# Batch 2's attention: strided head pairs in float32 groups first, then local head pairs in float16 units, on another timetable

## The chip, the core and the metric

The kernel runs on one core of one Trainium2 chip. The metric is the device time of one execution in microseconds (us), the median of several runs of the same program. The engines are TensorE (PE, with its weight loads as PEld), VectorE (DVE), ScalarE (ACT), GpSimd (POOL) and SyncE (SP), whose queue issues nearly all DMA transfers. Each works through its instructions in the order in which the program put them on it, and waits on semaphores for the others.

## The reference

Three stages follow each other, for 4 batches of 576 tokens and 512 channels:

```
scores = q @ k.T / 8                              # 8 heads of 64 channels
mask   = heads 0-3 (local):   0 <= row - col < 32
         heads 4-7 (strided): row >= col and row % 32 == col % 32
x = softmax(where(mask, scores, -1e9)) @ v        # heads side by side: 512 channels
h = relu(x @ w_in); u, v = halves of h            # gated unit
x = (u * (w_spatial @ layernorm(v) + b_spatial)) @ w_out
theta = x @ w_theta                               # token mixing
y = w_tok_r @ (x * cos(theta)) + w_tok_i @ (x * sin(theta))
u = x + y;  out = u + relu(u @ w_ch)
```

Results are float32. The kernel holds most operands as a pair of float16 numbers (a high part and what is left) and multiplies them in three passes.

## The kernel before

**The main line.** For each batch, `main_v` multiplies x with the second half of w_in (PSUM tiles `v`), `main_mid` makes `u`, `sp`, `x` and `th` chunks, and `main_end` makes `y` and `c` chunks and sends the output. The order is v(0), mid(0), v(1), end(0), mid(1), v(2), end(1), mid(2), v(3), end(2), mid(3), end(3). Main PSUM tiles come from a pool of three. A `y` chunk is 54 matmuls of 288 columns and there are four; two first `c` chunks follow with 18 matmuls each before their last 6.

**Attention.** Batch 0's stands ahead of the main line. The attention of batches 1, 2 and 3 is given out in steps between pieces of the main line: a generator yields after each step, and `others` (called after each piece) takes the next step of batch b once the main line's nominal clock, counted in matmul columns, has passed `ATT_AT[b][0] + n * ATT_AT[b][1]`. `drain(b + 1)` takes all that is left before `main_v(b + 1)`.

There are two forms of it:

- `attention1` (float32, batches 1 and 2 before): 9 groups g0 to g8 of up to 4 local or 6 strided blocks. g0 to g4 are the local head pairs 0 and 1, g5 to g8 the strided pairs 2 and 3. A group has scores and mask (into bank `sc`), row maximum and difference (DVE, `st` and `sm`), exponential (ACT), transposes by PE (bank `av`), a copy to SBUF (ACT, `pT`), the product with v (bank `av`), a division (DVE), transposes (bank `sc`) and two evacuations into xT (ACT, DVE). A step s does the output of group s-3, the product of s-2, the scores of s and the transposes of s-1.
- `attention` (float16 pairs, batch 3 before): 11 units of 4 blocks, 6 local and 5 strided. `prep_qk` loads one head's q and k for a pair as float32 (`qs`, `ks`, one buffer each) and splits them into `qT` and `kT`; `kT` lies in the same two tiles `kts` (`kt_80`, `kt_81` in the order) as the float32 form's q and k. A unit has scores (`sc`), four masked minimum passes (DVE), four exponentials (ACT), a division, a split into `ph`, one DMA transpose, and three steps later the product (`av`).

`sc` and `av` are one PSUM bank each for all groups and units. `vT` has two buffers, shared by the float32 v tiles (`v_...`) and the float16 ones.

**What else is in the way.** While batch 0's end runs, the weights w_ch are still being converted (`xT<-in_w_ch_dram`, ACT and DVE `wx`, POOL `wch`), batch 1's rows are normalised (`rs`, `vr`, `vn` on DVE and ACT), and the rotated values of batch 0 are transposed by DMA (`zf<-vn`). Main evacuations have a priority of 200 over attention work when a scheduler sets each engine's order; it is fixed in the program.

All instructions are recorded under one helper line (L103), so the rows below are told apart by tile names.

Of the kernel before, what the change touches and what calls it, by code (L numbers as in the profile page):

```python
# [32 lines left out]
N32 = 3  # L33
# [18 lines left out]
E_YHI = 'vaavvaav'  # L52
E_ZLO = 'vvvvvvvv'
WARM = 6
ATT_AT = (None, (2.7, 3.9), (79.0, 5.4), (169.9, 4.6))
CONV_SP = (20.0, 9.9, 1.9)
CONV_OUT = (37.0, 12.0, 5.0)
CONV_TH = (49.0, 12.0, 5.0)
# [7 lines left out]
def kernel(  # L66
# [52 lines left out]
    nc = Engines  # L119
    B, DM, S = out.shape  # L120
# [28 lines left out]
    def copy(eng, key, dst, src):  # L149
        e = eng[key]  # L150
        if key == "a":
            e.activation(dst, src, AF.Copy)
        else:
            e.tensor_copy(dst, src)
# [170 lines left out]
    units = []  # L325
# [4 lines left out]
    NU = len(units)  # L330
# [7 lines left out]
    def prep_qk(b, hp, j, tiles):  # L338
        local = hp < 2
        nk = S + STRIDE if local else S  # L340
        if j == 0:
            qT = att_p.tile([P, 2, S], F16, tag="qT", name="qT", bufs=2)
            kT = kts[hp % 2].rearrange("p j n -> p (j n)").bitcast(F16).rearrange("p (e j n) -> p e j n", e=2, j=2)
            tiles[hp] = qT, kT
        qT, kT = tiles[hp]
        qs = att_p.tile([P, S], F32, tag="qs", name="qs")
        nc.sync.dma_start(qs, qd[b - N32, hp, :, j, :])
        ks = att_p.tile([P, S + STRIDE], F32, tag="ks", name="ks")
        nc.sync.dma_start(ks[:, 0:nk], (kl_d[b - N32, hp] if local else ks_d[b - N32, hp - 2])[:, j, :])
        copy(N, E_QHI, qT[:, j], qs)  # L350
        nc.vector.tensor_tensor(qT[64:P, j], qs[64:P], qT[64:P, j], ALU.subtract)
        copy(N, E_KHI, kT[:, 0, j, 0:nk], ks[:, 0:nk])
        N[E_KLO].tensor_tensor(kT[:, 1, j, 0:nk], ks[:, 0:nk], kT[:, 0, j, 0:nk], ALU.subtract)

    def prep_v(ld):
        vs, nb = ld
        vT = att_p.tile([P, 2, 6, 2, 64], F16, tag="vT", name="vT", bufs=2)
        nc.scalar.activation(vT[:, 0, 0:nb], vs[:, 0:nb], AF.Copy, scale=VSC)
        nc.vector.scalar_tensor_tensor(vT[:, 1, 0:nb], vs[:, 0:nb], VSC, vT[:, 0, 0:nb],
                                       op0=ALU.mult, op1=ALU.subtract)  # L360
        return vT
# [65 lines left out]
    NG = len(groups)  # L427

    def load_qk(b, hp, q, k, c0, c1, by=None):
        by = by or nc.sync  # L430
        local = hp < 2
        src = kzl[b, hp] if local else kzs[b, hp - 2]
        k0, k1 = (c0 + STRIDE if c0 else 0, c1 + STRIDE) if local else (c0, c1)
        by.dma_start(q[:, c0:c1], qp[b, hp][:, c0:c1])
        for j in range(2):
            h = slice(64 * j, 64 * j + 64)
            by.dma_start(k[h, k0:k1], src[h, j, k0:k1])

    def load_vl(b, hp, v):
        src = vl_d[b, hp].rearrange("p n j d -> p n (j d)")  # L440
        c = slice(1, VW - 1)
        nc.gpsimd.memset(v[:, 0:9, 0:VW:VW - 1], 1.0)
        nc.sync.dma_start(v[0:96, 0:9:3, c], src[0:96, 0:6:2])
        nc.sync.dma_start(v[0:64, 1:9:3, c], src[64:128, 0:6:2])
        nc.sync.dma_start(v[64:96, 1:9:3, c], src[32:64, 1:6:2])
        nc.sync.dma_start(v[0:96, 2:9:3, c], src[32:128, 1:6:2])
# [211 lines left out]
            for f in end:  # L658
                f()

    def attention1(b):
        q, k, v = {}, {}, {}

        def load_a(hp):
            q[hp], k[hp] = kts[hp % 2][:, 0], kts[hp % 2][:, 1]
            load_qk(b, hp, q[hp], k[hp], 0, S)

        def load_b(hp):
            v[hp] = att_p.tile([P, 9, VW], F32, tag="vT", name="v32", bufs=2)
            if hp < 2:  # L670
                load_vl(b, hp, v[hp])
            else:
                load_vs(b, v[hp][:, 0:6].unsqueeze(1), (hp,))

        load_a(0)
        load_b(0)
        yield
        load_a(1)
        load_b(1)
        loads = {4: (load_a, 2), 6: (load_b, 2), 7: (load_b, 3)}  # L680
        un, xs = {}, {}
        for s in range(NG + 3):
            if s < NG:
                sm = att_p.tile([P, 384], F32, tag="sm", name="sm", bufs=2)
                pT = att_p.tile([P, 4, P], F32, tag="pT", name="pT32", bufs=2)
                st = att_p.tile([P, 2, 6], F32, tag="st", name="st", bufs=4)
                un[s] = (sm, pT, st)
            if s >= 3:
                gr_out(b, s - 3, xs.pop(s - 3), pa("sc"))
            if 2 <= s < NG + 2:  # L690
                sm, pT, st = un.pop(s - 2)
                pv = pa("av")[:, 0:3 * VW].rearrange("p (i n) -> p i n", i=3)
                gr_pv(s - 2, v, pT, pv, st, pT)
                xs[s - 2] = pT
            if s < NG:
                sm, pT, st = un[s]
                sc = pa("sc")
                gr_scores(s, q, k, sc)
                gr_shift(s, sc, sm, st)
                gr_exp(s, sm)  # L700
            if s in loads:
                f, hp = loads[s]
                f(hp)
                if s == 4:
                    load_a(3)
            if 1 <= s <= NG:
                sm, pT, st = un[s - 1]
                gr_turn(s - 1, sm, pa4("av"), pT)
            yield
# [34 lines left out]
                                     pT[:, pe, 2 * i + j, r0:r0 + R], start=(e == 0), stop=(e == 2))  # L744
        x_evac(xT[b % 2], spans_of(u), av)

    def attention(b):
        qk, vts, pTs = {}, {}, {}
        lv = load_v(b, 0)
        prep_qk(b, 0, 0, qk)  # L750
        yield
        prep_qk(b, 0, 1, qk)
        vts[0] = prep_v(lv)
        yield
        cur = None
        qk_at = {0: (1, 0), 1: (1, 1), 3: (2, 0), 4: (2, 1), 6: (3, 0), 7: (3, 1)}
        v_at = {2: 1, 5: 2, 8: 3}
        for s in range(NU + LAG16):
            if s + 1 in v_at:
                lv = load_v(b, v_at[s + 1])  # L760
            if s >= LAG16:
                att_pv(b, s - LAG16, pTs.pop(s - LAG16), vts)
            if 1 <= s <= NU:
                pTs[s - 1] = att_norm(b, cur)
            if s < NU:
                cur = att_scores(s, qk)
            if s in qk_at:
                prep_qk(b, *qk_at[s], qk)
            if s in v_at:
                vts[v_at[s]] = prep_v(lv)  # L770
            yield


# [271 lines left out]
    timed(list(sq_parts(wth, w_th)) + [switch], *CONV_TH)  # L1045
    timed([lambda i=i: tok_part(i, (raw2, raw1)[i // 2 % 2]) for i in range(0, NZ, 2)], *CONV_TOK)
    timed(sq_parts(wch, w_ch), *CONV_CH)
    atts = [None] + [attention1(b) for b in range(1, N32)] + [attention(b) for b in range(N32, B)]
    att = {"b": 1, "n": 0}

    def now():
        return clock[0] / 2400.0

    def step():
# [4 lines left out]
        att["n"] += 1  # L1059
        return True  # L1060

    def others():
        while conv and conv[0][0] <= now():
            conv.pop(0)[1]()
        while att["b"] < B and ATT_AT[att["b"]][0] + att["n"] * ATT_AT[att["b"]][1] <= now():
            step()

    def drain(b):
# [126 lines left out]
```

## Time and the profile before

| | |
|---|---|
| median of 3 runs | 505.43 us (505.38 to 506.62) |
| the profiled execution's own time | 506.96 us |
| its span, first to last instruction | 505.1 us |
| TensorE's granted clock, mean | 0.996 of full speed |
| PE busy | 485.1 us (96%) |
| DVE, ACT, POOL busy | 284.8, 267.8, 92.9 us |

The profile was taken on one execution, and its span is what the rows below add up to. PE is busy nearly all the time, so its rows in order of time show what each piece of attention takes out of the main line: the start of one row less the start of the row ahead of it. In `xcount` a float32 matmul of scores or of the product with v counts twice.

### The profile page before, as it was taken

Reading aid. Unit: us, or ns where it says so; the run is one execution under the profiler, and the core shown is the slowest. Engines: PE = TensorE matmul, PEld = TensorE weight load, DVE = VectorE, ACT = ScalarE, POOL = GpSimd, SP = SyncE. Lnnn points to the kernel's source line nnn. Section 1 sums busy time; section 2 is a strip of 40 time slices with the busy share of each in tenths; the row PEclk is TensorE's granted clock in tenths of the full one; section 3 lists DMA queues with packets and bytes.
Section 4 is the critical chain, followed back from the end, with each engine's and each line's share of the span. In section 5 each row is a group of like instructions: output and inputs, shape, how many; then the busy total and the mean of one; then the engine's idle time right before and its main releaser. Section 6 shows DMA issues by size and latency. Waiting matters only on the chain. (4 is left out here: it accounts for less than half of the span.)

```text
span 505.1 us, 10834 instructions
## 1 busy us (share of the span) xinstructions
PE 485.1 (96%) x4460; PEld 364.4 (72%) x4460; DVE 284.8 (56%) x607; ACT 267.8 (53%) x475; POOL 92.9 (18%) x91
## 2 busy tenths in 40 slices
PE   7889989998999999999999989999999999999996
PEld 5655757776567777888758867777657777777774
DVE  3765986555699343473499578772587121227412
ACT  2657788587994233345672757754862022149202
POOL 2042147225124400021003210021005200210220
PEclk9999999999899999999999999999999999999999
DMA  6868748377691024221080156230160020003402
GB/s 177 279 203 234 260 151 270 103 185 225 188 223 49 1 66 150 72 80 27 1 185 4 31 128 195 47 60 5 38 151 1 1 95 1 0 2 80 111 1 93
DMA packets 71788, 52.72 MB, mean 104 GB/s; under 512 B 50552, under 2 KB 59960, under 8 KB 71738
## 3 DMA queue, kind: packets, MB, share of 16 engines
q1 hardware_dynamic: 71434, 51.42, 36.5%
q8 instruction: 35, 0.57, 0.5%
q10 hardware_dynamic: 304, 0.61, 0.4%
q14 instruction: 15, 0.12, 0.1%
HBM read 35.36 MB, written 4.72 MB: 79 GB/s over the span
## 5 line engine op out<-in xcount | busy, mean ns | idle before, releaser
L103 PE MATMUL y<-wtok,zf 128*128 128x288 f16 x864 | 107.2, 286 | 1.0 <-DMA zf<-vn 1.0
L103 PEld LDWEIGHTS <-zf 128*128 128x128 f16 x864 | 84.1, 98 | 23.5 <-DMA zf<-vn 1.3
L103 PE MATMUL sp<-wsp,vn 128*128 128x288 f16 x384 | 52.2, 286 | 1.6 <-ACT vn L103 1.3
L103 PE MATMUL c<-x2h,wch 128*128 128x288 f16 x384 | 49.3, 286 | 2.3 <-ACT o L103 2.3
L103 PE MATMUL th<-x2h,wth 128*128 128x288 f16 x384 | 49.6, 291 | 2.0 <-DVE ta L103 2.0
L103 PE MATMUL x<-zf,wout 128*128 128x288 f16 x384 | 49.9, 286 | 0.0
L103 PE MATMUL u<-xT,win 128*128 128x288 f16 x384 | 49.7, 286 | 0.0
L103 PE MATMUL v<-win,xT 128*128 128x512 f16 (+1 forms) x240 | 48.4, 380 | 0.8 <-DVE xT L103 0.6
L103 PEld LDWEIGHTS <-vn 128*128 128x128 f16 x416 | 39.7, 98 | 12.1 <-ACT vn L103 1.4
L103 POOL TENSOR_TENSOR x2h<-x2f,x2h 128x576 f16<-128x576 f32 x20 | 25.5, 1279 | 119.1 <-ACT x2h L103 47.2
L103 PEld LDWEIGHTS <-wth 128*128 128x128 f16 x384 | 38.1, 100 | 12.5 <-issue 2.2
L103 PEld LDWEIGHTS <-wch 128*128 128x128 f16 x384 | 37.3, 98 | 11.8 <-issue 2.7
L103 PEld LDWEIGHTS <-win 128*128 128x128 f16 x384 | 37.3, 98 | 9.2
L103 PEld LDWEIGHTS <-wout 128*128 128x128 f16 x384 | 36.7, 98 | 9.6
L103 PEld LDWEIGHTS <-xT 128*128 128x128 f16 (+1 forms) x240 | 21.0, 100 | 25.2 <-issue 2.2
L103 ACT ACTIVATE x2h<-x2f 128x576 f16<-128x576 f32 (+1 forms) x28 | 20.9, 746 | 28.9 <-DVE x2f L103 28.4
L103 DVE SCALAR_TENSOR_TENSOR x2f<-y,x2f 128x576 f32<-128x576 f32 x16 | 12.0, 753 | 30.6 <-PE y L103 30.5
L103 DVE TENSOR_TENSOR u<-u,sp 128x576 f32<-128x576 f32 x16 | 12.0, 752 | 28.2 <-PE sp L103 28.2
L103 ACT ACTIVATE o<-c 128x576 f32<-128x576 f32 (+1 forms) x17 | 10.4, 616 | 32.1 <-PE c L103 31.8
L103 DVE TENSOR_TENSOR ta<-ta,x2f 128x1152 f32<-128x1152 f32 x16 | 21.5, 1354 | 9.8 <-ACT ta L103 9.8
L103 POOL TENSOR_TENSOR zf<-u,zf 128x576 f16<-128x576 f32 x8 | 10.7, 1340 | 86.0 <-ACT zf L103 86.0
L103 DVE TENSOR_TENSOR vn<-ta,vn 128x1152 f16<-128x1152 f32 x16 | 21.5, 1355 | 5.6 <-ACT vn L103 5.6
(140 smaller groups left out, 738.2 us busy)
## 6 DMA issues: line engine op xcount, KB each, us to landing
out_dram<-o SPq DMA_DIRECT2D x15, 288.0 KB
kt<-in_qp_dram SPq DMA_DIRECT2D x8, 288.0 KB
qs<-in_qd_dram SPq DMA_DIRECT2D x8, 288.0 KB
x2f<-in_w_in_dram SPq DMA_DIRECT2D x2, 1024.0 KB
zf<-in_w_in_dram SPq DMA_DIRECT2D x2, 1024.0 KB
xT<-in_w_ch_dram SPq DMA_DIRECT2D x2, 1024.0 KB
kt<-in_kzl_dram SPq DMA_DIRECT2D x8, 152.0 KB
ks<-in_kl_dram SPq DMA_DIRECT2D x4, 304.0 KB
```

The lines of the kernel that those rows point to most:

```text
L103: ins = f(*args, **kwargs)
```

## The change

`attention2` replaces `attention1` for batch 2. It starts `attention1` at group 5 (so only the four strided groups are left), and runs `attention` with 6 units (so only the local ones). A string says whose step is next. The timetable of batch 2 begins at 77.0 instead of 79.0; the first 11 steps are 3.1 apart, the others 5.0, where all were 5.4 apart before. q and k of the local pairs are loaded from the arrays of the float32 form, in two halves of 64 partitions.

```diff
-ATT_AT = (None, (2.7, 3.9), (79.0, 5.4), (169.9, 4.6))
+ATT_AT = (None, (2.7, 3.9), (77.0, 3.1, 11, 5.0), (169.9, 4.6))
...
-        nc.sync.dma_start(qs, qd[b - N32, hp, :, j, :])
+        if b < N32:
+            h = slice(64 * j, 64 * j + 64)
+            for e in range(2):
+                nc.sync.dma_start(qs[64 * e:64 * e + 64], qp[b, hp, h])
+        else:
+            nc.sync.dma_start(qs, qd[b - N32, hp, :, j, :])
...
+            for e in range(2):
+                nc.sync.dma_start(ks[64 * e:64 * e + 64, 0:nk],
+                                  (kzl[b, hp] if local else kzs[b, hp - 2])[h, j, :])
...
-    def attention1(b):
+    def attention1(b, g0=0):
...
+        if g0:
+            load_a(2)
+            load_b(2)
+            yield
+            load_a(3)
+            loads = {g0 + 1: (load_b, 3)}
...
-        for s in range(NG + 3):
+        for s in range(g0, NG + 3):
...
-    def attention(b):
+    def attention(b, NU=NU):
...
+    def attention2(b):
+
+        strided, local = attention1(b, NG - 4), attention(b, 6)
+        for c in "sssssls" "lsls" "llllllll":
+            next({"s": strided, "l": local}[c])
             yield
...
-    atts = [None] + [attention1(b) for b in range(1, N32)] + [attention(b) for b in range(N32, B)]
+    atts = [None, attention1(1), attention2(2)] + [attention(b) for b in range(N32, B)]
...
+    def at(first, gap, n=99, late=0.0):
+
+        return first + min(att["n"], n) * gap + max(att["n"] - n, 0) * late
...
-        while att["b"] < B and ATT_AT[att["b"]][0] + att["n"] * ATT_AT[att["b"]][1] <= now():
+        while att["b"] < B and at(*ATT_AT[att["b"]]) <= now():
```

Where the instructions go is set by the scheduler. Three places follow.

ACT, from batch 1's normalised rows (`vn`) on, while batch 0's y chunks run on PE. Before, `pT_1928` and `pT_1984` are the copies of g0 and g1:

```order
L103 ACTIVATE vn<-vr_1715 128x2x512
L103 ACTIVATE x2h<-x2f 128x576 x2
L103 ACTIVATE pT_1928<-av 96x512
L103 ACTIVATE sm<-sm 128x384
L103 ACTIVATE pT_1984<-av 96x512
L103 ACTIVATE sm<-sm 128x384
L103 ACTIVATE xT_94<-sc 128x256
```

ACT at the same place now; `pT_1891` and `pT_1932` are the copies of g5 and g6, `kt` and `qT` the splits of the local pairs' k and q:

```order
L103 ACTIVATE vn<-vr_1715 128x2x512
L103 ACTIVATE x2h<-x2f 128x576
L103 ACTIVATE pT_1891<-av 128x384
L103 ACTIVATE kt_80<-ks 128x608
L103 ACTIVATE qT<-qs 128x576
L103 ACTIVATE sm<-sm 128x384
L103 ACTIVATE kt_81<-ks 128x608
L103 ACTIVATE pT_1932<-av 128x384
L103 ACTIVATE sm<-sm 128x384
L103 ACTIVATE qT<-qs 128x576
L103 ACTIVATE xT_94<-sc 128x18x18
```

Two splits of freshly loaded k now stand ahead of copies and exponentials for which PE waits; the second (`kt_81<-ks`) stands directly ahead of the copy of g6.

DVE at that place now, from the evacuation of g6's scores on (`st<-sc` and `sm<-sc,st`):

```order
L103 TENSOR_REDUCE st<-sc 128x6
L103 TENSOR_TENSOR sm<-sc,st 128x384
L103 TENSOR_TENSOR kt_80<-ks,kt_80 128x608
L103 TENSOR_TENSOR qT<-qs,qT 64x576
L103 TENSOR_SCALAR st<-av 128x6
L103 RECIPROCAL st<-st 128x6
L103 TENSOR_TENSOR pT_1891<-av,st 128x384
L103 TENSOR_REDUCE st<-sc 128x6
L103 TENSOR_TENSOR sm<-sc,st 128x384
L103 TENSOR_TENSOR kt_81<-ks,kt_81 128x608
L103 TENSOR_TENSOR qT<-qs,qT 64x576
L103 SCALAR_TENSOR_TENSOR x2f<-y_1971,x2f 128x576
```

`kt_80<-ks,kt_80` is the last reader of the one `ks` buffer, so the load that `kt_81<-ks` needs can only be issued behind it. After these rows comes `xT_94<-sc,xT_94`, the last reader of g5's output in bank `sc`.

SP, from the rotated values' first transpose (`zf<-vn`) to w_ch's second load (`xT_94<-in_w_ch_dram`). Before, six transposes stood ahead of that load with nothing between them. Now:

```order
L103 DMA_TRANSPOSE zf<-vn 128x9x128
L103 DMA v_1951<-in_vs_dram 54x128
L103 DMA_TRANSPOSE zf<-vn 128x9x128
L103 DMA v_1951<-in_vs_dram 54x128
L103 DMA v_1951<-in_vs_dram 20x128
L103 DMA v_1951<-in_vs_dram 34x128
L103 DMA v_1951<-in_vs_dram 54x128
L103 DMA_TRANSPOSE zf<-vn 128x9x128 x4
L103 DMA v_1951<-in_vs_dram 38x128
L103 DMA v_1951<-in_vs_dram 16x128
L103 DMA v_1951<-in_vs_dram 54x128 x3
L103 DMA_TRANSPOSE zf<-vn 128x9x128
```

Ten small loads of strided v (`v_1951`) and one more transpose have moved ahead of w_ch's second load.

## Rows read from the trace of the kernel before

**Rows 1.** The page's first part: busy time, share of the span, instructions.
```profile
PE 485.1 (96%) x4460; PEld 364.4 (72%) x4460; DVE 284.8 (56%) x607; ACT 267.8 (53%) x475; POOL 92.9 (18%) x91
```
**Rows 2.** PE's waits: engine, tile, releaser: us in total, times, longest.
```profile
PE c L103 <- ACT o L103: 2.3, 2, 1.7
```
**Rows 3.** Timeline of PE, batch 2's float32 local groups: start, us, what.
```profile
162.04 0.88 PE L103 MATMUL sc<-kt 64*64 64x96 f32 x16
...
163.47 6.78 PE L103 MATMUL y<-wtok,zf 128*128 128x288 f16 x54
170.17 0.74 PE L103 MATMUL av<-v,pT 96*64 96x65 f32 x16
170.84 0.88 PE L103 MATMUL sc<-kt 64*64 64x96 f32 x16
...
176.67 0.38 PE L103 MATMUL sc<-ident,pT 128*128 128x128 f32 x2
176.98 0.73 PE L103 MATMUL av<-v,pT 96*64 96x65 f32 x16
```
**Rows 4.** Timeline of PE, batch 3's float16 local units.
```profile
275.21 0.61 PE L103 MATMUL sc<-kt,qT 128*96 128x128 f16 x8
275.66 4.57 PE L103 MATMUL y<-wtok,zf 128*128 128x288 f16 x36
...
289.87 0.45 PE L103 MATMUL av<-pT,vT 128*64 128x96 f16 x12
290.25 0.65 PE L103 MATMUL sc<-kt,qT 128*96 128x128 f16 x8
```
**Rows 5.** A window of batch 3's attention: PE, PEld, DVE, ACT, POOL, clock, DMA.
```profile
312.00:322.00 10.00, 10.00 (x109) 7.87 (x107) 7.10 (x28) 6.93 (x24) 0.00 (x0) 1.00 0.52 111
```
**Rows 6.** Timeline of PE: batch 0's y, and strided groups of batch 2.
```profile
142.10 20.02 PE L103 MATMUL y<-wtok,zf 128*128 128x288 f16 x162
...
210.15 0.33 PE L103 MATMUL sc<-mask,identb 128*128 128x384 bf16 x1
...
211.25 0.55 PE L103 MATMUL av<-ident,sm 128*128 128x128 f32 x3
211.64 2.37 PE L103 MATMUL sp<-wsp,vn 128*128 128x288 f16 x18
...
217.76 0.49 PE L103 MATMUL sc<-ident,pT 128*128 128x128 f32 x3
218.18 0.96 PE L103 MATMUL av<-v,pT 54*64 54x65 f32 x24
```
**Rows 7.** Timeline of SP's queue: issues; of small v loads, w_ch, ks in batch 3.
```profile
87.89 9.47 SPq L103 DMA_DIRECT2D v<-in_vs_dram  x26
...
144.40 0.40 SPq L103 DMA_DIRECT2D xT<-in_w_ch_dram  x1
...
289.83 0.37 SPq L103 DMA_DIRECT2D ks<-in_ks_dram  x1
```
**Rows 8.** Timeline of ACT: conversion of w_ch's second half; exponential; ks in batch 3.
```profile
150.10 1.16 ACT L103 ACTIVATE xT<-xT 128x1024 f32<-128x1024 f32 x1 [0.60 <-DMA xT<-in_w_ch_dram]
...
165.69 0.51 ACT L103 ACTIVATE sm<-sm 128x384 f32<-128x384 f32 x1
...
292.82 0.68 ACT L103 ACTIVATE kt<-ks 128x576 f16<-128x576 f32 x1 [0.80 <-DMA ks<-in_ks_dram]
```
**Rows 9.** Timeline of DVE, batch 1's normalisation to g0's scores; POOL's wch.
```profile
155.17 2.27 POOL L103 TENSOR_TENSOR wch<-wx,wch 128x512 f16<-128x512 f32 x2 [2.25 <-ACT wch L103]
155.30 1.04 DVE L103 SCALAR_TENSOR_TENSOR rs<-rs 128x5 f32<-128x5 f32 x1
...
158.50 2.36 DVE L103 TENSOR_SCALAR vr<-vr,mv,rs 128x512 f32<-128x512 f32 x5
...
163.71 0.75 DVE L103 SCALAR_TENSOR_TENSOR x2f<-y,x2f 128x576 f32<-128x576 f32 x1
...
164.96 0.56 DVE L103 TENSOR_TENSOR sm<-sc,st 128x384 f32<-128x384 f32 x1
```

More of the change, by code (lines that the diff above doesn't have):

```diff
@@ L346, in prep_qk @@
         qs = att_p.tile([P, S], F32, tag="qs", name="qs")
-        nc.sync.dma_start(qs, qd[b - N32, hp, :, j, :])
-        ks = att_p.tile([P, S + STRIDE], F32, tag="ks", name="ks")
-        nc.sync.dma_start(ks[:, 0:nk], (kl_d[b - N32, hp] if local else ks_d[b - N32, hp - 2])[:, j, :])
+        if b < N32:
[4 more added lines that the diff above has]
+            nc.sync.dma_start(qs, qd[b - N32, hp, :, j, :])
+        ks = att_p.tile([P, S + STRIDE], F32, tag="ks", name="ks")
+        if b < N32:
+            for e in range(2):
+                nc.sync.dma_start(ks[64 * e:64 * e + 64, 0:nk],
+                                  (kzl[b, hp] if local else kzs[b, hp - 2])[h, j, :])
+        else:
+            nc.sync.dma_start(ks[:, 0:nk], (kl_d[b - N32, hp] if local else ks_d[b - N32, hp - 2])[:, j, :])
         copy(N, E_QHI, qT[:, j], qs)
@@ L673, in load_b @@
                 load_vs(b, v[hp][:, 0:6].unsqueeze(1), (hp,))
[L675 to L680, printed above, removed]
+        if g0:
[4 more added lines that the diff above has]
+            loads = {g0 + 1: (load_b, 3)}
+        else:
+            load_a(0)
+            load_b(0)
+            yield
+            load_a(1)
+            load_b(1)
+            loads = {4: (load_a, 2), 6: (load_b, 2), 7: (load_b, 3)}
         un, xs = {}, {}
-        for s in range(NG + 3):
+        for s in range(g0, NG + 3):
             if s < NG:
@@ L687, in attention1 @@
                 un[s] = (sm, pT, st)
-            if s >= 3:
+            if s >= g0 + 3:
                 gr_out(b, s - 3, xs.pop(s - 3), pa("sc"))
-            if 2 <= s < NG + 2:
+            if g0 + 2 <= s < NG + 2:
                 sm, pT, st = un.pop(s - 2)
@@ L705, in attention1 @@
                     load_a(3)
-            if 1 <= s <= NG:
+            if g0 + 1 <= s <= NG:
                 sm, pT, st = un[s - 1]
@@ L758, in attention @@
         for s in range(NU + LAG16):
-            if s + 1 in v_at:
+            if s + 1 in v_at and units[s + 1][0][0] < units[NU - 1][0][0]:
                 lv = load_v(b, v_at[s + 1])
@@ L766, in attention @@
                 cur = att_scores(s, qk)
-            if s in qk_at:
+            if s in qk_at and qk_at[s][0] <= units[NU - 1][0][0]:
                 prep_qk(b, *qk_at[s], qk)
-            if s in v_at:
+            if s in v_at and v_at[s] <= units[NU - 1][0][0]:
                 vts[v_at[s]] = prep_v(lv)
+            yield
+    def attention2(b):
+        strided, local = attention1(b, NG - 4), attention(b, 6)
+        for c in "sssssls" "lsls" "llllllll":
+            next({"s": strided, "l": local}[c])
             yield
```

## The prediction

> **What bounds the kernel now.** I read the page's first part, PE's waits, then PE's timeline over batch 2's attention, and only then the queues that feed it. PE is busy for 96% of the span [rows 1], and its longest single wait on ACT in the middle of the run is 1.7 us [rows 2]. While batch 2's attention runs, PE's rows follow each other without idle brackets [rows 3, 6]. So whatever a piece of attention takes on PE is added to the end of the run, at its full length, and work on DVE, ACT, POOL and the DMA queue counts only where PE comes to wait for it. The reader is to see in rows 3 that each piece of attention stands between main matmuls, and that its price is the start of the next row less its own start.
>
> **What goes from PE.** A local float32 group costs 163.47 - 162.04 = 1.43 us for scores, mask and transposes, 170.84 - 170.17 = 0.67 for the product with v, and 176.98 - 176.67 = 0.31 for the transposes of its output [rows 3]: 2.41 us. Four of them are 9.64. The fifth, g4, has two blocks of four: at least half, 1.2, at most 2.41; half its instructions are of the same forms, so I take 1.3. Sum 10.9.
>
> **What comes to PE.** A local float16 unit costs 275.66 - 275.21 = 0.45 for scores and 290.25 - 289.87 = 0.38 for the product [rows 4]; its transposes are DMA. Six units: 5.0. PE's work falls by 5.9 us, with the bounds 5.8 and 7.0. The strided groups keep their matmuls and only change place.
>
> **What comes to the other engines.** The six units bring masked passes, exponentials, splits and the loads' conversion to DVE and ACT. In batch 3's window with the same kind of units beside u and sp chunks, DVE is busy 7.10 of 10 us, ACT 6.93, and PE 10.00 [rows 5]; so I cost them at nothing where batch 2's units stand beside u and sp. PE's work is the cover. If it fails there, the pattern is PE's wait of 1.7 us on ACT beside batch 3's c chunks [rows 2], the same price again. The extra loads (q and k in two copies) go on a queue that has time in that stretch.
>
> **Where the gain is partly given back.** The place is batch 0's y. Before, g0's scores came early, and g0's transposes only after three y chunks (162 matmuls from 142.10 to 162.04, 0.123 us each) [rows 3, 6]. Now the steps are 3.1 apart, so g5's product, g6's and g7's scores fall beside the third chunk, and g8's early in the fourth. Without any wait PE would go: two chunks, 108 x 0.123 = 13.3, to 155.4; g6's scores and mask as 211.25 - 210.15 = 1.10; g5's transposes 0.39 (211.64 - 211.25); 36 y matmuls 4.4; g5's product some 0.9 (0.96 with its overlapping end) [rows 6]. That reaches g7's scores at 162.2. Then 1.10, two y matmuls 0.25, transposes 0.39, 16 y 1.97, g5's output 0.42 (218.18 - 217.76), g6's product 0.9, 4 y 0.49 [rows 6]: g8's scores at 167.7.
>
> What PE needs on that way hangs on one time, X: the end of DVE's evacuation of g6's scores (`sm<-sc,st`). g7's scores need the bank that this frees. From X on, the new order on DVE and ACT is a chain through one buffer: the split of `ks` on DVE, which I price as the 576-column pass of 0.75 [rows 9], frees it; the next load is issued, and lands 292.82 - 289.83 = 3.0 us later [rows 7, 8]; ACT's `kt_81<-ks` takes 0.68, and the copy behind it, for which g6's product waits, about 0.51 like the exponential [rows 8]. So the copy is there at X + 4.9. Behind it on ACT come an exponential (0.51) and `qT<-qs` (0.68), to X + 6.1, then on DVE the rest of qT (0.75), a y evacuation (0.75) and the evacuation of g5's output (about 0.5), which frees bank `sc` for g8's scores at X + 8.1. What PE waits in all is X + 8.1 - 167.7 = X - 159.6.
>
> X from rows of before: the same evacuation (of g0) ended at 164.96 + 0.56 = 165.5, which is 15.4 us after ACT began on w_ch's second load at 150.10 [rows 8, 9]. DVE's order ties the two: w_ch's pass stands in the middle of the normalisation. Three things change. (1) That load was issued at 144.40; now ten more small v loads stand ahead of it at 9.47 / 26 = 0.36 us of issue each [rows 7], 3.6 us at most, nothing where the queue was idle anyway; I take the middle, 1.8. (2) One y evacuation and one q split no longer stand ahead, 0.75 each by the row of the first [rows 9]. (3) The small `rs` passes took 158.50 - 155.30 = 3.2 us [rows 9] for eight of them behind w_ch's pass; now six stand ahead of it, where DVE waits for ACT anyway: 0 to 2.8 less, and I take 2.4. X = 150.1 + 1.8 + 15.4 - 1.5 - 2.4 = 163.4, and PE's waits there are 3.8 us. The bounds are 150.1 + 15.4 - 1.5 - 2.8 = 161.2 (waits of 1.6) and 150.1 + 3.6 + 15.4 - 1.5 = 167.6 (waits of 8.0).
>
> The 3.0 us of a load is a row of this trace. The Trainium skill (DMA: Bandwidth & Descriptors, Anatomy of one DMA) gives a fixed part of about 2.0 us and the bytes at 436 GB/s, fitted on another issue path; an estimate by that page for one of these loads of 304 KB is 2.7 us, and would make the time 0.3 us shorter.
>
> Other waits: the ten v loads also stand among the transposes of the rotated values, whose first pair y needs at 142.1. I cost that at 0.3 for what is left over, with 0 and 2 as ends.
>
> **The sum.** -5.9 on PE, +3.8 waits at y, +0.3: -1.8 us. The profiled execution had a span of 505.1 and a time of 506.96, 1.5 above the median of 505.43: its span would become 503.3, its time 505.1, and the median 503.6.
>
> **The rivals.**
> - *The waits don't come, the whole gain stays.* For: PE had no idle time here, and the units run beside full PE in batch 3 [rows 5]. Against: ACT's order puts a split that waits for a load straight ahead of the copy for g6. If w_ch's load is no later and the small passes go as (3) at its best, X = 161.2: 505.4 - 5.9 + 1.6 = 501.1, and without waits 499.5.
> - *A draw.* The forecast's waits, and once more a wait of 1.7 us as in rows 2, where batch 0's last c chunks meet the first unit: 503.6 + 1.7 = 505.3. For: bank `sc` goes from g7's output to unit 0's scores to g8's output within some 12 c matmuls there. Against: DVE has little else at that place.
> - *Slower: normalisation and w_ch's conversion collide.* One mechanism: POOL's two `wch` passes (2.27 us) fell beside the `rs` passes before, and a pass of five columns took 1.04 us there; now they fall beside the five `vr` passes (2.36 us without company) [rows 9]. If these are held up for all of POOL's 2.27, and the load is late by its full 3.6, X = 163.4 + 2.3 + 1.8 = 167.5, waits 7.9, and the time 505.4 - 5.9 + 7.9 + 0.3 = 507.7. It decides from X = 165.2 on, where waits eat the gain. Against: at 158.5 the vr passes ran undisturbed, and part of the collision is already in the 15.4.
>
> The last is also what a page has: the Trainium skill (GPSIMD Engine Reference, its table of specifications) says that POOL shares its SBUF interfaces with VectorE, with contention for some of VectorE's instruction forms. The row of 1.04 agrees; how far it goes for `vr` no row here shows.
>
> **How the numbers follow.** About 0.3% (1.5 us) is what a measurement of this kernel can tell from no change: faster is below 503.9, slower above 506.9. The forecast (X near 163.4, within 1.5 us) has 0.42, the whole gain 0.20, the draw 0.20, the collision 0.18. Of the forecast's share about 0.30 lies below 503.9 and 0.12 above; the whole gain's 0.20 lies below; of the draw's share 0.17 stays within the 1.5 us and 0.03 goes over, where its waits come on top of a late X; of the collision's 0.15 lies above 506.9 and 0.03 within. That is faster 0.50, same 0.32, slower 0.18. The range leaves out the case without any wait (499.5) and the collision at its full price (507.7), about one in ten on each side: 500.3 to 506.9; the forecast's own range is 501.9 to 505.3.
>
> **What would show it.** Right: in the new trace the local part takes PE about 5 us in six pairs of 0.45 and 0.38; PE shows idle brackets at g5's or g6's product and at g8's scores, together 3 to 5 us, released by ACT's copy and by DVE; ahead of the copy for g6 ACT waits for `ks`; before 142 and after u begins nothing changes. Wrong: PE idle at the first y matmul (the transposes came late), idle of more than 2 us in the u, sp or x stretch of batch 1, or float16 units that cost PE clearly more than 0.83 us.

## The result, and the profile after

| | before | after |
|---|---|---|
| median of 4 runs each | 505.74 us (505.38 to 506.62) | 509.02 us (507.83 to 509.17) |
| ratio, 95% interval | | 1.0058 [1.0034, 1.0082] |
| the profiled execution: time, span | 506.96, 505.1 us | 509.17, 507.4 us |

The change makes the kernel 0.6% slower. The forecast was 503.6 us, and its range ended at 506.9.

From the page of after, the busy times, and PE's busy share and granted clock in 40 slices of 12.7 us:

```profile
PE 480.8 (95%) x4402; PEld 361.2 (71%) x4402; DVE 301.8 (59%) x664; ACT 282.9 (56%) x529; POOL 94.3 (19%) x89
...
PE   7889989998995899999999989999999999999996
...
PEclk9999999999999699999999999999999999999999
```

PE has less to do than in [rows 1] (480.8 for 485.1 us) and DVE and ACT more, and still the span grew by 2.3. The 13th digit of PE's line, 5, and the 14th of the clock's, 6, say where: between 152 and 178 us, at batch 0's y.

PE's timeline of after there and further on (start, us, instructions; in brackets the idle time before and what ended it) answers to [rows 3, 4, 6]:

```profile
140.53 13.40 PE L103 MATMUL y<-wtok,zf 128*128 128x288 f16 x108
153.77 0.33 PE L103 MATMUL sc<-mask,identb 128*128 128x384 bf16 x1
...
155.16 4.57 PE L103 MATMUL y<-wtok,zf 128*128 128x288 f16 x36
164.88 1.62 PE L103 MATMUL av<-v,pT 54*64 54x65 f32 x24 [5.15 <-ACT pT L103]
167.78 0.48 PE L103 MATMUL sc<-mask,identb 128*128 128x384 bf16 x1 [1.28 <-DVE sm L103]
...
171.06 3.19 PE L103 MATMUL y<-wtok,zf 128*128 128x288 f16 x16
...
176.26 0.27 PE L103 MATMUL sc<-mask,identb 128*128 128x256 bf16 x1 [0.19 <-DVE xT L103]
...
196.47 0.61 PE L103 MATMUL sc<-kt,qT 128*96 128x128 f16 x8
196.92 1.63 PE L103 MATMUL c<-x2h,wch 128*128 128x288 f16 x12
...
214.78 0.45 PE L103 MATMUL av<-pT,vT 128*64 128x96 f16 x12
215.16 0.65 PE L103 MATMUL sc<-kt,qT 128*96 128x128 f16 x8
...
252.81 11.94 PE L103 MATMUL v<-win,xT 128*128 128x512 f16 x60
```

Two things are to be seen. PE now waits in a stretch where before shows no wait at all, from the start of y to v(2): 5.15 us at g5's product, 1.28 at g7's scores, 0.19 at g8's. And behind the long wait the same matmuls take longer: 16 y matmuls need 174.09 - 171.06 = 3.03 us for 16 x 0.123 = 1.97, g5's product 1.62 for 0.96. The windows of after over this stretch give the reason in the seventh figure, the granted clock:

```profile
core 0: us, PE busy (x) PEld busy (x) DVE busy (x) ACT busy (x) POOL busy (x), PEclk, DMA share, GB/s
160.00:165.00 5.00, 0.12 (x2) 0.12 (x4) 4.94 (x6) 3.99 (x6) 3.35 (x3) 0.80 0.00 0
165.00:170.00 5.00, 3.72 (x51) 2.91 (x51) 4.83 (x8) 1.52 (x3) 2.81 (x2) 0.50 0.03 5
170.00:175.00 5.00, 4.93 (x39) 3.46 (x39) 2.80 (x5) 2.40 (x5) 0.00 (x0) 0.68 0.40 120
```

0.50 is the lower of TensorE's two levels, 1.2 for 2.4 GHz. The clock fell while PE stood idle ahead of 164.88 and came back within the third window: 0.20 x 5 x 2 + 5 + 0.32 x 5 x 2 = 10.2 us at the lower level, part of them idle. PE's pieces in it took 3.3 us more than the same pieces at full clock.

**The account.** From the start of batch 0's y to the start of v(2), the stretch that holds all of batch 2's attention, before took 250.10 - 142.10 = 108.00 us and after 252.81 - 140.53 = 112.28. Of these 6.6 are PE's waits and 3.3 the lower clock; what is left, 102.4, is PE's work: 5.6 less than before. So +4.3 in this stretch. Ahead of it after is 1.6 us shorter, since `th` chunks behind a wait of 2.02 us ran at the lower clock in the profiled execution of before (0.66 in the window from 125 to 130) and at 1.00 behind one of 1.86 in that of after; behind it 0.5 shorter. Sum +2.2, the span's 2.3. The 1.6 at `th` are a difference between two single executions; the medians differ by 3.3.

PE's timeline of before at `th` and at v(2), then that of after at `th`:

```profile
125.73 4.66 PE L103 MATMUL th<-x2h,wth 128*128 128x288 f16 x24 [2.02 <-DVE ta L103]
...
250.10 11.94 PE L103 MATMUL v<-win,xT 128*128 128x512 f16 x60
```
```profile
125.72 3.10 PE L103 MATMUL th<-x2h,wth 128*128 128x288 f16 x24 [1.86 <-DVE ta L103]
```

What the waits hang on stands on the other queues of after; these rows answer to [rows 7 to 9]. The timelines are SP's queue (the issues of w_ch's second load and of `ks`), then ACT, DVE and POOL:

```profile
148.40 0.53 SPq L103 DMA_DIRECT2D xT<-in_w_ch_dram  x1
...
168.48 1.11 SPq L103 DMA_DIRECT2D ks<-in_kzl_dram  x2
```
```profile
154.02 1.15 ACT L103 ACTIVATE xT<-xT 128x1024 f32<-128x1024 f32 x1 [3.80 <-DMA xT<-in_w_ch_dram]
...
161.37 2.01 ACT L103 ACTIVATE vn<-vr 128x1024 f16<-128x1024 f32 x2 [0.66 <-DVE vr L103]
...
164.34 0.49 ACT L103 ACTIVATE pT<-av 128x384 f32<-128x384 f32 x1
172.15 0.71 ACT L103 ACTIVATE kt<-ks 128x608 f16<-128x608 f32 x1 [3.87 <-DMA ks<-in_kzl_dram]
172.77 0.47 ACT L103 ACTIVATE pT<-av 128x384 f32<-128x384 f32 x1
```
```profile
157.75 4.33 DVE L103 TENSOR_SCALAR vr<-vr,mv,rs 128x512 f32<-128x512 f32 x5
...
163.51 3.16 DVE L103 TENSOR_TENSOR vn<-vr,vn 128x1024 f16<-128x1024 f32 x1
...
167.17 0.56 DVE L103 TENSOR_TENSOR sm<-sc,st 128x384 f32<-128x384 f32 x1
```
```profile
158.61 2.45 POOL L103 TENSOR_TENSOR wch<-wx,wch 128x512 f16<-128x512 f32 x2 [5.10 <-ACT wch L103]
163.46 2.13 POOL L103 TENSOR_TENSOR vn<-vr,vn 128x1024 f16<-128x1024 f32 x1 [1.65 <-ACT vn L103]
```

The `vn` passes of before, of DVE and of POOL:

```profile
162.58 1.22 DVE L103 TENSOR_TENSOR vn<-vr,vn 128x1024 f16<-128x1024 f32 x1
```
```profile
162.58 3.20 POOL L103 TENSOR_TENSOR vn<-vr,vn 128x1024 f16<-128x1024 f32 x1 [1.26 <-ACT vn L103]
```

Read the rows of after backwards from g5's product. ACT's copy of g5's transposes (164.34) stands in its queue behind batch 1's normalised values `vn`, these behind DVE's five `vr` passes, and these took 4.33 us beside POOL's two `wch` passes for 2.36 alone [rows 9]; the `vn` pass that follows took 3.16 beside POOL's share of the same work, which took 2.13 (in before it was POOL's share that took longer: 3.20, and DVE's pass 1.22). The evacuation of g6's scores stands on DVE behind that pass; g5's copy doesn't wait for it. Ahead of all that ACT had waited 3.80 us for w_ch's load. Lower down, the copy of g6 (172.77) stands behind a split that waited 3.87 for `ks`.

### The profile page after: what moved, and what is told of

Same layout as the page of the kernel before. It is cut to its first block, busy times and chain, and to the rows that moved or that the text cites. A ratio compares the mean times of both kernels' runs of the same rounds, so it can differ in the third digit from the quotient of the medians.

```text
span 507.4 us, 10844 instructions
## 1 busy us (share of the span) xinstructions
PE 480.8 (95%) x4402; PEld 361.2 (71%) x4402; DVE 301.8 (59%) x664; ACT 282.9 (56%) x529; POOL 94.3 (19%) x89
## 5 line engine op out<-in xcount | busy, mean ns | idle before, releaser
L103 PE MATMUL y<-wtok,zf 128*128 128x288 f16 x864 | 109.3, 288 | 1.1 <-DMA zf<-vn 1.1
L103 POOL TENSOR_TENSOR x2h<-x2f,x2h 128x576 f16<-128x576 f32 x20 | 26.6, 1328 | 127.2 <-ACT x2h L103 40.0
L103 PE MATMUL th<-x2h,wth 128*128 128x288 f16 x384 | 48.2, 286 | 1.9 <-DVE ta L103 1.9
L103 PEld LDWEIGHTS <-wth 128*128 128x128 f16 x384 | 37.4, 98 | 11.3 <-issue 1.8
L103 PEld LDWEIGHTS <-wch 128*128 128x128 f16 x384 | 37.2, 98 | 11.5 <-issue 2.3
L103 ACT ACTIVATE sm<-sm,st 96x128 f32<-96x128 f32 (+1 forms) x68 | 26.6, 394 | 10.0 <-DVE st L103 9.9
```

Of the source, the lines that this page charges most:

```text
L103: ins = f(*args, **kwargs)
```

## The experiments

Each ratio is to runs of before made beside it. y to v is the stretch of the account (before 108.0, after 112.3; not given for e8, where units fall beyond it). It is read from one execution, and that one can lie off its median: by 2 to 3 us below in e8 and e9, by 1.6 to 2.1 above in e2, e7 and e12, by at most 1.2 either way in before and the others. A difference of 1 or 2 us in that column is therefore not established. Where a kernel has a line added above the helper, the helper is L104.

| | median us | ratio to before, 95% | y to v |
|---|---|---|---|
| after | 509.02 | 1.0058 [1.0034, 1.0082] | 112.3 |
| e1_later | 514.56 | 1.0162 [1.0124, 1.0199] | 116.8 |
| e2_fill | 516.12 | 1.0194 [1.0160, 1.0228] | 117.2 |
| e3_order | 519.78 | 1.0247 [1.0207, 1.0288] | 120.0 |
| e4_wch_behind | 507.38 | 1.0021 [0.9994, 1.0048] | 109.2 |
| e5_held | 512.01 | 1.0119 [1.0082, 1.0155] | 111.7 |
| e6_held_fill | 511.46 | 1.0099 [1.0061, 1.0136] | 109.1 |
| e7_held_later | 511.04 | 1.0094 [1.0057, 1.0132] | 108.0 |
| e8_held_pace | 508.72 | 1.0045 [1.0015, 1.0075] | |
| e9_hold2 | 508.35 | 1.0038 [1.0015, 1.0062] | 110.9 |
| e10_hold2_later | 506.26 | 1.0001 [0.9980, 1.0022] | 107.5 |
| e11_hold2_last | 502.12 | 0.9922 [0.9892, 0.9952] | 103.7 |
| e12_hold2_wch_first | 506.55 | 0.9982 [0.9950, 1.0013] | 109.5 |

**e3_order: the place without the units.** Batch 2 keeps float32 groups throughout, the strided ones first, at the new place.

```
-ATT_AT = (None, (2.7, 3.9), (77.0, 3.1, 11, 5.0), (169.9, 4.6))
+ATT_AT = (None, (2.7, 3.9), (77.0, 3.1, 5, 5.4), (169.9, 4.6))
-atts = [None, attention1(1), attention2(2)] + ...
+atts = [None, attention1(1), attention1(2, (5, 6, 7, 8))] + ...
```

> The order of groups alone: batch 2 with strided groups first as in the changed kernel (first steps at the same times), but the local groups in float32 as before, 5.4 apart. PE has none of the 5.9 us saved. Theory T (the place of the strided groups at y costs what the changed kernel lost, some 9 us): the idle time of about 5 us at g5's product is there again, then the half clock or waits behind it; 511 to 515 us. Without the units' loads the copy for g6 does not stand behind a split of ks, so the lower half of that is likelier. Rival U (the float16 units cost the time): no loss at y worth more than 2 us, 504.5 to 507.5.

PE's timeline of e3:

```profile
164.97 1.62 PE L103 MATMUL av<-v,pT 54*64 54x65 f32 x24 [5.65 <-ACT pT L103]
...
169.14 0.48 PE L103 MATMUL sc<-mask,identb 128*128 128x384 bf16 x1 [2.55 <-DVE sm L103]
```

The waits of after are here, at the same instructions and larger, without one float16 unit, and y to v is 12 us longer than before. The place costs without the units, which refutes rival U; how much, the theory put too low (519.78 for 511 to 515).

**e1_later: the strided steps later.** Only the timetable is changed.

```
-ATT_AT = (None, (2.7, 3.9), (77.0, 3.1, 11, 5.0), (169.9, 4.6))
+ATT_AT = (None, (2.7, 3.9), (84.0, 3.1, 11, 4.4), (169.9, 4.6))
```

> The changed kernel with batch 2's pieces given out later: the first at 84.0 for 77.0, the last five 4.4 apart for 5.0. g6's scores now stand behind three of batch 0's y chunks instead of two, g5's product half a chunk into the fourth. Theory T (the float16 units save their 5.9 us, and the strided groups lose them at y, where PE asks for g5's product 5.15 us before the exponentials' transposes are copied): the same chain on DVE and ACT is over when PE asks, g5's product is asked for at 25.8 us after y's start instead of 19.2, and the chain delivered it at 24.4; so idle at y is under 1.5 us, the clock stays, and the time is 500 to 502.5 us. Rival U (the units themselves cost the time, by DVE's and ACT's extra 17 and 15 us of work, wherever the strided groups stand): 506 to 509.

Both theories missed. PE's timeline of e1, and ACT's:

```profile
173.88 1.62 PE L103 MATMUL av<-v,pT 54*64 54x65 f32 x24 [7.90 <-ACT pT L103]
```
```profile
171.46 0.68 ACT L103 ACTIVATE qT<-qs 128x576 f16<-128x576 f32 x1 [6.97 <-DMA qs<-in_qp_dram]
...
173.34 0.49 ACT L103 ACTIVATE pT<-av 128x384 f32<-128x384 f32 x1
```

The wait at g5's product is longer, and has another cause: the program now has the second local pair's split of q ahead of g5's copy on ACT, and that split waits 6.97 us for a load issued only when DVE's pass had freed the one buffer `qs` (168.0 us). So a second thing that the change brought, float32 loads through single buffers into in-order queues, can cost more than the first.

**e2_fill: PE kept busy with 36 unused matmuls ahead of g5's product**, to see what the clock's fall is worth.

```
+                if g0 and s == g0 + 2:
+                    fill = pm("fill")
+                    for _ in range(FILL):          # FILL = 36
+                        nc.tensor.matmul(fill[:, 0, 0:HS], win[:, 0, 0, 0:P], win[:, 0, 0, 0:HS], start=True, stop=True)
```

> The changed kernel with 36 matmuls of 288 columns whose result nobody reads, ahead of g5's product: 36 x 0.123 = 4.4 us of work in the 5.15 us that PE stood idle there. They should keep the clock at 2.4 GHz, where the changed kernel shows half of it for 10.2 us behind that idle time, at a loss of 3.3 us. Theory T (PE is held at y by the chain that begins with DVE's evacuation of g6's scores and ends 8.1 us later with bank sc for g8's scores, whatever PE's speed): the clock stays, but the 3.3 us come back as idle time at g6's product and g8's scores; 508.3 to 509.5. Rival C (the clock's fall is a price of its own on top of the waits): 505.0 to 506.5.

Both missed again: the clock did stay at 1.00 through the product (165 to 170), but the edit moved the same split of q ahead of g6's copy on ACT, with 5.33 us of wait for its load, PE waited 6.95 us at g6's transposes, and the clock fell behind that wait (0.50 from 175 to 180). Nothing follows on the clock.

**e4_wch_behind: w_ch's conversion due 8 us later on the timetable.**

```
-CONV_CH = (87.0, 14.1, 4.8)
+CONV_CH = (87.0, 6.1, 4.8)
```

> The changed kernel with one number of the timetable changed: w_ch's conversion is due 8 us later, so the pass on its second half stands behind g6's evacuation on DVE, and ACT's passes on it behind the normalised values. Theory T (X, the end of g6's evacuation, is late since w_ch's late second load stands in the middle of the normalisation on DVE and ACT, and its POOL passes beside DVE's): X comes 4 to 7 us earlier against y's start (20 to 23 us for 27.2), idle at y is 1 to 4 us, no long stretch at half clock, and the time is 501.5 to 504.5. Rival N (the normalisation itself, or g6's scores, set X; w_ch's load only fills time in which DVE waits anyway): X within 2 us of 27.2, time 507.5 to 509.5.

Rows of e4, of PE and of DVE:

```profile
164.13 1.62 PE L103 MATMUL av<-v,pT 54*64 54x65 f32 x24 [3.81 <-ACT pT L103]
```
```profile
162.34 0.56 DVE L103 TENSOR_TENSOR sm<-sc,st 128x384 f32<-128x384 f32 x1
```

The evacuation of g6's scores ends 162.90 - 141.12 = 21.8 us after y's start, near what the prediction had (21.3) and 5.4 before that of after (27.2). So w_ch's load and its passes are what made it late in after. But the wait at g5's product only fell from 5.15 to 3.81, and y to v by 3.1: other passes of the conversion (`xT` 1.12 and `wx` 1.10 us) now stood on ACT ahead of g5's copy, and others lengthened the way from there to g8's scores (174.15 - 162.90 = 11.3 us for 8.5 in after). The time missed the theory's range (507.38 for 501.5 to 504.5) and the ratio is not clear of no change. This is the run to keep in mind for the prediction: with that evacuation within 0.5 us of its forecast place, the kernel was still 3.8 us above the forecast of 503.6.

**e5_held and e6_held_fill: all local splits of q and k held behind g8's copy**, the strided steps all first; and the same with the 36 matmuls of e2.

```
+    def held(ins, b):                  # keeps ins behind the last group's copy in the order
+        if b < N32:
+            tc.add_manual_dep(ins.ins, turned[-1], ...NoSync...)
-        copy(N, E_QHI, qT[:, j], qs)
+        held(copy(N, E_QHI, qT[:, j], qs), b)      # k alike
-        for c in "sssssls" "lsls" "llllllll":
+        for c in "ssssssss" "lllllllllll":
```

> The changed kernel, with ACT's splits of the local units' q and k held behind the last strided group's copy (g8's), so that no load of q or k stands ahead of a strided group's copy on ACT or evacuation on DVE; PE's order up to g7's output is that of the changed kernel. In e1 ACT stood 6.97 us for a load of q ahead of g5's copy, in e2 5.33 us ahead of g6's. Theory L (two things hold PE at y: first the normalisation ahead of g5's copy, then the loads ahead of g6's): the wait at g5's product stays at about 5 us, and that at g7's scores at 1.3; the half clock behind the first (3.3 us) stays, and it hides what the loads would cost; 507.5 to 509.5. Rival X (the evacuation of g6's scores alone sets all waits, loads add nothing, as the prediction had it up to X): the same time. Rival A (the loads are the whole loss): 504 to 505.5. This run is the base of the next.

> The same with the 36 idle-time matmuls (4.4 us) ahead of g5's product, and no other difference in any engine's order. Without loads in the way, theory L has the clock stay at 2.4 GHz, idle of 0.7 us at g5's product and 1 to 2.5 at g7's scores, and the time 2 to 3.5 us under e5_held's, 504.5 to 506.5. Rival W (PE is held by DVE and ACT whatever its own speed, the clock's fall is hidden): within 1 us of e5_held.

In total both missed upward. Ahead of y the `th` chunks waited 2.4 us for 1.9 in after, and ran at the lower clock behind that (24 matmuls 4.77 and 5.92 us for 3.10). By the medians, e6 is 0.55 us below e5, which is not clear of noise and is what rival W had. Within y to v the two traces can be compared. PE's timeline and a window (the clock is the figure ahead of the last two) of e5, then the same of e6:

```profile
165.82 1.62 PE L103 MATMUL av<-v,pT 54*64 54x65 f32 x24 [3.64 <-ACT pT L103]
```
```profile
165.00:170.00 5.00, 2.90 (x41) 2.42 (x43) 4.45 (x6) 1.27 (x3) 3.74 (x2) 0.50 0.00 0
```
```profile
169.25 0.97 PE L104 MATMUL av<-v,pT 54*64 54x65 f32 x24
```
```profile
165.00:170.00 5.00, 5.00 (x59) 3.97 (x57) 4.94 (x5) 2.49 (x4) 3.60 (x2) 1.00 0.00 0
```

With 36 x 0.123 = 4.4 us of unused work in the place of the idle time, y to v is 2.6 us shorter; 0.7 of that is a wait at a unit's scores, far behind y, that only e5's trace has. PE does more and is done sooner there, with the clock at its upper level. That the lower clock behind an idle stretch is a price of its own, where no load stands in the way, is thus seen in one trace of each and not in the medians.

**e7_held_later, e8_held_pace: e5's hold with other timetables**, (84.0, 3.1, 8, 3.9) and (79.0, 5.4, 5, 3.8).

> The splits held as in e5_held, and the pieces given out at e1_later's times (first at 84.0, the local ones 3.9 apart): e1_later, but with no load ahead of a strided group's copy. Theory L (e1's 7.9 us at g5's product were the load of q on ACT; without it the copy stands ready 24.4 us after y's start, and PE asks at 25.8): idle at y under 2 us, clock at 2.4 GHz, 499.5 to 502.5 us. Rival N (the normalisation itself came later with the later pieces): the wait of 5 to 8 us is there again, 508 to 514.

> The splits held, and the strided pieces at the pace of the kernel before (first at 79.0, 5.4 apart, the local ones 3.8 apart behind them): g5's product stands behind batch 0's whole y, where the kernel before has its first. Theory L: no wait at y at all, the 5.9 us of PE's work stay; the local units fall on x, th and v of batch 1, where one of them may wait a microsecond; 499 to 502. Rival U (the float16 units cost the time wherever they stand): 505 or more.

Both did away with the waits at y, as expected, and neither was faster: the times are those of the rivals, though in e7 the wait that its rival named is gone. In e7 the local units, all late now, met the main line elsewhere (three waits of their scores for DVE, 2.3 us in all, and three of their products, 1.9), and `th` waited as in e5. PE's row of one of them:

```profile
219.91 0.61 PE L103 MATMUL sc<-kt,qT 128*96 128x128 f16 x8 [1.10 <-DVE st L103]
```

In e8's trace PE waits 2.83 us for DVE within v(2), but that execution was its fastest (505.71) and below before's, so it doesn't show what its median of 508.72 is made of. A hold on all splits was no cure in either.

**e9_hold2, e10_hold2_later, e11_hold2_last: only the second local pair's splits held**, with the timetable of the changed kernel, of e1, and a later one.

```
+    def held(ins, b, hp):
+        if b < N32 and hp == 1:
+            tc.add_manual_dep(ins.ins, turned[HOLD], ...NoSync...)     # HOLD = -1
e10: ATT_AT[2] = (84.0, 3.1, 11, 4.4)      e11: ATT_AT[2] = (88.0, 2.6, 11, 4.4)
```

> The changed kernel with only the second local head pair's splits of q and k (hp 1) held behind g8's copy on ACT; the order of every engine up to g7's output is that of the changed kernel, but for the loads. e5 had held the first pair's too, which had been done early, beside u, and lost time ahead of y for it. Theory L: the waits of 5.2 at g5's product and 1.3 at g7's scores and the half clock behind them (3.3 us) stay, and the wait for the load behind them (3.87 us on ACT) had been hidden by them: 507.5 to 509.5. Rival A (the loads are the whole loss): 503 to 505.5.

> e1_later with the second pair's splits held in the same way: nothing else differs from e1. Theory L: e1's wait of 7.9 us at g5's product goes, and its half clock with it, so y takes some 31.6 us as in e7 and not 43.3, and the rest goes as in e1 (73.5 us from c to batch 1's v); y to v is 105 us, against 108.0 in the kernel before and 112.3 in the changed one: 502 to 505. Rival U (DVE and ACT are too full for the units wherever the strided groups stand; e7 lost 5 us in sp and x): 507 to 511.

> The same with the strided pieces later still: first at 88.0, 2.6 apart, so that g5's product stands behind all of batch 0's y, as the kernel before's first one does. Theory L: no idle at y, but four strided groups 2.6 apart in c, where one or two may wait a microsecond for DVE: 502 to 506. Rival U: 507 to 511.

PE's timeline of e9 at g5's product and g8's scores, of e10 at g5's product, and of e11 there and at the waits behind it:

```profile
163.19 1.10 PE L104 MATMUL av<-v,pT 54*64 54x65 f32 x24 [4.68 <-ACT pT L104]
...
173.44 0.27 PE L104 MATMUL sc<-mask,identb 128*128 128x256 bf16 x1
```
```profile
168.38 0.97 PE L104 MATMUL av<-v,pT 54*64 54x65 f32 x24 [2.33 <-ACT pT L104]
```
```profile
169.51 0.97 PE L104 MATMUL av<-v,pT 54*64 54x65 f32 x24 [0.26 <-ACT pT L104]
170.93 0.32 PE L104 MATMUL sc<-mask,identb 128*128 128x384 bf16 x1 [0.45 <-DVE sm L104]
...
173.14 0.52 PE L104 MATMUL av<-ident,sm 128*128 128x128 f32 x3 [0.45 <-DVE pT L104]
```

At the changed kernel's own place the hold does next to nothing, as theory L had it (e9: 508.35 for 509.02, not clear of noise, though g6's copy no longer waits for `ks` and g8's scores no longer wait at all). At e1's place it is worth 8.3 us (e10 for e1), a little less than e10's expectation asked for (506.26 for 502 to 505). And where g5's product and g7's scores come behind the whole of batch 1's normalisation (e11, within its expected range), the waits at y shrink to 1.2 us, the clock stays up, and the kernel is 0.8% faster than before: the version that beats both. Its y to v without its waits is 103.65 - 1.16 = 102.5 us, 5.5 less than before's 108.0: PE's saving was there all the time. DVE's `vr` passes took 4.34 us in e11 too, so it is the later place that did away with the waits, and not a milder collision. All six units are in it, and so it also answers rival U: the units don't cost the time wherever they stand.

**e12_hold2_wch_first: e9 with w_ch's second load issued ahead of the small v loads.**

```
+        with tc.high_priority(1000 if src is w_ch else 0):
+            ins = nc.sync.dma_start(pair(stg, c.stop - c.start), ...)
+                    if hps == (3,) and b == 2 and i >= 1:
+                        tc.add_manual_dep(ins.ins, wch_loads[-1], ...NoSync...)
```

> e9_hold2 with w_ch's second load put ahead of nearly all of g6's small v loads in the DMA queue, right behind the fourth pair of transposes, where the kernel before has it; the orders of PE, ACT and POOL are those of e9, and DVE's but for the load's own pass. In the changed kernel that load was issued at 148.4 and ACT waited 3.8 us for it in the middle of the normalisation. Theory L (the ten v loads ahead of it make X late): it is issued 3 to 5 us earlier against y's start, ACT's wait for it goes to under 1 us, g5's copy comes 2 to 3.5 us earlier (20.9 to 22.4 us after y's start for 24.4), idle at g5's product is 1.5 to 3 us, the clock may then stay, and the time is 503 to 506.5. Rival K (X is late by POOL's passes beside DVE's five vr passes, 4.33 us for 2.36, which then only come earlier together; or by the normalisation as such): idle at g5's product stays at 4 us or more, 507.5 to 509.5.

Rows of e12, of PE, DVE and POOL:

```profile
166.56 1.62 PE L104 MATMUL av<-v,pT 54*64 54x65 f32 x24 [5.09 <-ACT pT L104]
```
```profile
157.53 0.37 DVE L104 TENSOR_TENSOR rs<-rs 128x5 f32<-128x5 f32 x2
...
158.74 2.14 DVE L104 TENSOR_TENSOR rs<-rs 128x5 f32<-128x5 f32 x2
...
161.12 2.36 DVE L104 TENSOR_SCALAR vr<-vr,mv,rs 128x512 f32<-128x512 f32 x5
```
```profile
158.58 2.27 POOL L104 TENSOR_TENSOR wch<-wx,wch 128x512 f16<-128x512 f32 x2 [4.02 <-ACT wch L104]
```

The load was issued 5.3 us after y's start for 7.9 in after, and ACT still waited 2.77 us for it. The five `vr` passes are back at 2.36 us. But POOL's passes now meet two passes of five columns each, 2.14 us where two such took 0.37 just before, and g5's copy comes 23.75 us after y's start for 23.8 in after. In this trace the collision is moved and not removed, which is what rival K said, with 5.09 us of idle time at g5's product; the 1.4 us gained in y to v on e9 came behind, at g7's scores, which no longer wait. The time lies between the two ranges: 506.55, by the ratios 0.6% faster than e9 and no slower than before. So the earlier load is worth something, more than the rival allowed, and the one trace, of an execution 1.6 us above its median, doesn't show all of it.

## Why the prediction was wrong

- **PE's saving of 5.9: right.** Measured 5.6 in after and 5.5 in e11. The six units stand in pairs of 0.45 (196.92 - 196.47) and 0.38 (215.16 - 214.78), as priced.
- **DVE's and ACT's work for the units at nothing: right where it was claimed**, beside u and sp. In after PE has no wait from g8's scores to v(2), where the units stand.
- **The way of PE without waits: right.** g5's product was to be reached 161.3 - 142.1 = 19.2 us after y's start; 159.73 - 140.53 = 19.2.
- **The chain behind X: right in length.** X is the end of DVE's evacuation of g6's scores. From X to the end of g6's copy 5.5 us (4.9 predicted), to g8's scores 8.5 (8.1). The wait of `ks`'s split ahead of g6's copy is there, with 3.87.
- **X itself: this is the term that failed.** The prediction put X at 163.4, 21.3 us after y's start. It came at 167.73, 27.2 after. Of the 5.9 us in between, w_ch's load accounts for 2.1 (ACT began on it at 154.02, 3.9 later than in [rows 8], for the "middle" of 1.8 and a bound of 3.6; the ten v loads took 3.8 us of issue, and the transpose that moved ahead with them, which the bound had left out, 1.3, while 1.1 of the queue's idle time was used up). The way from ACT's first pass of w_ch to X was longer by 2.2: 13.7 for 15.4 - 1.5 - 2.4 = 11.5. In that, `vr` beside POOL's `wch` is 2.0 and `vn` beside POOL's `vn` 1.9; 1.7 go off it, 1.0 of them since more of the small `rs` passes had been done early than priced (ten, not eight, stood behind w_ch's pass in before, and two do in after). The last 1.6 is that y began earlier in the traced execution while the load did not. The choice of the middle and of an undisturbed `vr` was the error: both went to the other end together. That is the third rival, to which I gave 0.18. That its X of 167.5 is so near 167.73 is in part luck: it had neither the hold-up of `vn` nor the larger saving on `rs`.
- **The first wait was left out: the second step that failed.** The signs named g5's product, but the working took it at "some 0.9" without a wait and let PE's whole loss hang on X and g6's chain. g5's copy stands on ACT behind `vn`, and so on the same late normalisation, but not behind X: 5.15 us, the largest wait. In e4 a nearly right X was not enough: X at 21.8 us after y's start, near the forecast's 21.3, and still 3.81 us at g5's product and 507.38 us in all. It is no clean test, since the conversion's passes stand elsewhere in the same chain. e9 shows it from the other side: the chain from X through `ks` is cut, and g8's scores, which no longer wait, come 173.44 - 139.31 = 34.1 us after y's start for 35.7 in after and 25.6 without any wait.
- **The clock was not in the sum.** The 10.2 us at the lower level cost 3.3 us on PE's pieces. How much of it is a price of its own in after stays open: X + 8.1 is 175.8, so the chain through `ks` alone would have held g8's scores to within 0.5 us of where they came (176.26). e9 has the chain gone and keeps the lower clock, and gains 1.4 in its trace; e6's trace is 2.6 shorter than e5's where the clock stays up and no load stands behind it. By these two readings, in after each covers for the other, and taking away one gives little.
- **"Nothing changes before 142 and after u": right** but for the clock at `th` in one execution of each and 0.5 us at the end.

By the prediction's own formula PE's loss from y's start to g8's scores is X + 8.1 - (167.7 - 1.6) = 167.7 + 8.1 - 166.1 = 9.7 us; measured 176.26 - 166.1 = 10.1. With that for 3.8, the sum is -5.9 + 9.7 + 0.3, or +4.1, for the +4.3 of the account. So the term for waits was too small by 6 us, and the late X gives its size. That the formula comes out is no proof of its path: in e9 the waits at g5's product and at g7's scores and the lower clock, without the chain through `ks`, take PE to g8's scores nearly as late, and are enough for a kernel slower than before.

POOL's collision has a rule beside it: the Trainium skill (SBUF — State Buffer, the section on SBUF's two separate sides) says that VectorE and GpSimd share a port pair under an exclusive lock, for a VectorE instruction with two SBUF inputs or in a 2-port mode, and that the loser blocks for the whole instruction. The traces agree in size: +1.97 us on `vr` beside two POOL passes of 2.45 together, +1.77 on `rs` in e12 beside two of 2.27. At `vn` the hold-up changed sides, from POOL in before to VectorE in after. The prediction also gave an estimate by the Trainium skill (DMA: Bandwidth & Descriptors, Anatomy of one DMA) of 2.7 us for a load of `ks`; in after, in two halves, it took 172.15 - 168.48 = 3.67 from issue to use, so the measurement decides, and the row of 3.0 was nearer.

## What to carry to other kernels

Before moving work to a place where PE has no idle time, list for each of its dependent steps what stands ahead of it on the in-order queues of the engines that serve it, the first step included, and ask what those passes wait for in their turn: a load behind a dozen small issues, or a pass that another engine holds up. Where several uncertain terms hang on one event, as both did on w_ch's load here, they go wrong together, so the far end deserves more than a small chance. When removing one cause gives little, look for a second one that covers for it before giving the theory up: here the hold alone gave 0.7 us (e9, not clear of noise), a later place alone lost 5.5 (e1), and the two together made the kernel faster than either (e10, and e11 a little later still).

## What the runs showed of the hardware

- After idle time of 3.64 to 5.65 us PE ran at its lower clock for the matmuls that followed (g5's product took 1.62 us in e5, e4, e12, after and e3), and the upper level came back some 10 us later in after. In e9 the product behind 4.68 us of idle time still took 1.10 us, nearly its full-clock 0.97, and the lower clock came right behind it. After 2.33 us in e10 g5's product took 0.97. In the stretch of `th`, idle time of 2.02 us (before) and 2.38 (e5) was followed by a lower clock (4.66 and 4.77 us for 24 matmuls), and 1.86 (after) was not (3.10).
- With such idle time filled with unused matmuls the clock stayed at 1.00, and the stretch was 2.6 us shorter in the one trace of each (e6 for e5); the medians don't tell the two apart.
- Beside each other, VectorE and POOL passes on data in SBUF were held up, in these cases by up to nearly the other's length, however small the pass: two VectorE passes of 5 columns took 2.14 us for 0.37 beside two POOL passes of 2.27 together (e12), five of 512 took 4.33 for 2.36 beside two of 2.45 (after). Which of the two loses changes: at `vn`, POOL took 3.20 and VectorE 1.22 in before, POOL 2.13 and VectorE 3.16 in after. Not every pass is held up: after's evacuation of g6's scores from PSUM took 0.56 beside a POOL pass, as it did in e12 and e4.
